# Result stores made events of their own in five buffers, and the order of all events written anew, in a fused attention and feed-forward kernel

## The chip, the cores and the metric

One core of one Trainium2 chip runs the whole program. The metric is the device time of one launch in microseconds (us), the median over several runs. Of one execution there is also a profile: what every engine (PE, DVE, ACT, POOL, SP) and every DMA queue did, and when.

## The reference

Two stages stand behind one another. The first is an attention over 8 batches, 8 heads, 576 positions and 64 channels, in a local and a coarse part that are added. The second is a feed-forward block over the 4608 = 8 x 576 tokens with 512 channels in, 2048 hidden and 512 out.

```python
q_d = q.reshape(B, H, Sd, 4, D).mean(axis=3)          # k_d and v_d likewise; Sd = 144
out_up = np.repeat(sm_attn(q_d, k_d, v_d), 4, axis=2) # softmax attention, each row four times
mask = np.abs(pos[:, None] - pos[None, :]) < 4        # the local band
scores = np.where(mask, scale * np.matmul(q, k.transpose(0, 1, 3, 2)), -1000000000.0)
attn = softmax(scores)
attn_out = out_up + np.matmul(attn, v)
x = attn_out.transpose(0, 2, 1, 3).reshape(4608, 512)
h = x @ w_in
g = np.where(h > 0.0, h, np.exp(np.minimum(h, 0.0)) - 1.0)
return g @ w_out
```

## The kernel before

The work is cut into some 1,280 small events, each a call of one short function that emits a few instructions. A table of words in the program, ORDER, lists the events in the order in which they are emitted; `run` first emits what an event depends on (its `after` list) and, where a buffer it takes is full (its `alloc` list, against the table CAP), the users of the oldest one. An engine executes its own instructions strictly in the order of emission, and waits at each for what it needs from the others. So ORDER decides what stands behind what on PE, DVE, ACT, POOL and SP.

The events' names have a letter code and indices: b is a batch of 0 to 7, j a pair of heads of 0 to 3, t a block of 512 tokens of 0 to 8, i a number within a block. For attention:

- `lq` and `lv` load q, k and v of a pair. SP issues `lq` (L321), except for batches 0 and 1, where POOL issues DMAs that also cast (L308), and SP issues the four DMAs of `lv` (L358). `cq` (L344) and `cv` (L386) cast to 16 bit on POOL, each with a tiny copy behind it (L333).
- `tr` transposes q and k of a pair on PE (L409 for batches 0 and 1, L414 after), and `eq`, `ek` evict them (L424, on ACT or DVE by a table). From batch 3 on k is transposed by a DMA instead, which SP issues: `fl` (L427).
- `sq` and `sk` sum q and k over four positions, on DVE (L443) or POOL (L447 and L452), by a table.
- `sc` are the scores (PE, L463 local, L473 coarse), `xl` and `xf` their exponentials (ACT, L483), `mk` the band's mask (DVE, L492), `dn` the denominators (PE, L508) and `rc` their reciprocal (DVE, L518).
- The reciprocals must be spread over partitions. Batches 0 to 2 do that with matmuls, `sp` (L549) and a copy `sx` (L556). Batches 3 to 7 send them through DRAM: `so` writes them out (L529, rd<-rc) and `si` reads them back spread (L535, rcb<-rd, two DMAs); SP issues both.
- `vs` and `vd` are sums of v on PE (L566) and their copy (L574), `out` and `far` the outputs on PE (L592, L611), `nm` the normalisation (DVE, L638 and L643), `ad` adds both parts into the block's input xt (L650, on POOL, or on DVE where the table `adv` says so).

For the feed-forward block:

- `m1` computes 128 hidden rows of a block, four 128x512 matmuls (L663); the first two of block 0 come in pieces, `mp`. `ex` (ACT, L683, or two passes L680 and L681 where the table `rl` says so) and `el` (DVE, L690, or L694 and L695) form the ELU into gt. `m2` are four matmuls of the second product (L708); sixteen of them make a block.
- `wi` and `wo` load a quarter each of the two weight matrices, issued by POOL (L286, L290). Quarter n of w_in serves the events `m1.0.4n` to `m1.0.4n+3` of block 0 and the same of later blocks.
- `cp` takes 128 finished rows: ACT copies them from PSUM to one of three buffers "os" (L716), and SP stores them (L718).

PE also runs matmuls on a tile of zeros, Z (L394), that compute nothing; a table `fill` says how many stand ahead of which event. PSUM gives two large slots (a third until `cf`), two "hp" for `m1` and two "misc" for `m2`, the vs and some of the denominators.

## Time and profile before

| | |
|---|---|
| time, median of 3 runs | 342.42 us (341.69 to 342.69) |
| the profiled execution's own time | 342.38 us |
| its span in the profile | 340.6 us |
| mean granted TensorE clock | 0.99 |
| PE busy in the span | 325.0 us (95%) |
| DVE, ACT, POOL busy | 230.7, 209.4, 156.5 us |

The span runs from the first to the last instruction that the profile shows; 1.78 us of the own time lie around it. "Busy" counts an engine's instructions, and a matmul stream at half the clock counts as busy too. Rows of a timeline give the start in us, the duration in us, the engine, the line of the program, the operation with its tiles, the count where neighbours are joined, and in brackets how long the engine had been idle and what released it. "SPq" is SP's queue, whose time is spent in issuing DMAs; the transfer itself goes on behind it. Rows by window give the stretch, then the busy time and count of PE, PEld, DVE, ACT and POOL, the granted clock as a share of full speed, the DMA engines' share and GB/s.

### The profile page before, as it was taken

The numbers are of one execution on the slowest core, as the hardware profiler recorded it, in microseconds if no ns is written. First come the engines' busy times: TensorE is split into PE (matmuls) and PEld (weight loads), VectorE is DVE, ScalarE is ACT, GpSimd is POOL, SyncE is SP. The second block draws the span as 40 slices with busy tenths as digits, with TensorE's granted clock in tenths as the row PEclk, the third lists the DMA queues.
The fourth block names the chain that finished last, engine by engine and source line by source line (L and its number), as shares of the span: only waits on it lengthen the run. The fifth ranks groups of instructions, "written<-read, shape, count | busy, mean of one in ns | idle before, by whom it ended". The sixth has DMA issues, their size and how long they took to land.

```text
span 340.6 us, 9762 instructions
## 1 busy us (share of the span) xinstructions
PE 325.0 (95%) x3976; PEld 169.8 (50%) x3976; DVE 230.7 (68%) x429; ACT 209.4 (61%) x365; POOL 156.5 (46%) x299
## 2 busy tenths in 40 slices
PE   6799979999999997999999999999999999999996
PEld 3355445555545553555555555555444444444443
DVE  2668998768778957788997966699775455443400
ACT  3544888888457862555676767765446646657621
POOL 6694765876795674857684347632011000000000
PEclk9879999999999999999999999999999999999999
DMA  8999999989887949999996996331310100000112
GB/s 168 195 180 227 168 248 224 196 196 155 214 149 165 232 114 179 249 199 224 166 251 152 162 239 169 115 88 69 89 64 31 63 34 31 31 33 31 56 70 92
DMA packets 99735, 48.66 MB, mean 143 GB/s; under 512 B 81130, under 2 KB 94698, under 8 KB 99690
## 3 DMA queue, kind: packets, MB, share of 16 engines
q1 hardware_dynamic: 93530, 41.57, 55.1%
q0 software_dynamic: 5600, 6.26, 11.4%
q8 instruction: 31, 0.51, 0.7%
q10 hardware_dynamic: 560, 0.21, 0.3%
q14 instruction: 14, 0.11, 0.1%
HBM read 41.66 MB, written 9.67 MB: 151 GB/s over the span
## 4 chain that ended last, share of the span: by engine, by line
PE 66%; DMA 15%; DVE 8%; ACT 3%; SPq 3%; issue 2%; POOL 1%; ACTq 0%; POOLq 0%; DVEq 0%
PE op L708 28%; PE hp L663 28%; DMA v<-in_v_dram 4%; DMA rcb<-rd 3%; DMA k<-in_k_dram 3%; DMA kt<-k 3%; DVE gt L695 2%; PE lg L592 2%; DVE rc L518 1%; SPq L427 1%; PE sc L463 1%; DVE e L694 1%; DVE ln L643 1%; DMA MASK<-MASKc 1%; PE den L508 1%
## 5 line engine op out<-in xcount | busy, mean ns | idle before, releaser
L663 PE MATMUL hp<-xt,WI 128*128 128x512 f16 x576 | 148.0, 380 | 2.5 <-DVE gt L695 2.2
L708 PE MATMUL op<-WO,gt 128*128 128x512 f16 (+2 forms) x592 | 145.3, 374 | 0.0
L663 PEld LDWEIGHTS <-WI 128*128 128x128 f16 x576 | 62.6, 114 | 57.3 <-issue 3.6
L708 PEld LDWEIGHTS <-gt 128*128 128x128 f16 x592 | 55.1, 98 | 60.2
L690 DVE SCALAR_TENSOR_TENSOR gt<-e,hp 128x512 f16<-128x512 f16 x71 | 48.4, 683 | 43.0 <-ACT e L681 42.6
L683 ACT ACTIVATE e<-hp 128x512 f16<-128x512 f32 x73 | 43.6, 599 | 41.5 <-PE hp L663 40.0
L680 ACT ACTIVATE r<-hp 128x512 f32<-128x512 f32 x71 | 42.6, 600 | 40.9 <-PE hp L663 40.5
L695 DVE SCALAR_TENSOR_TENSOR gt<-hp,e 128x512 f16<-128x512 f32 x73 | 50.5, 692 | 2.8
L650 POOL TENSOR_TENSOR xt<-ln 128x320 f16<-128x320 f16 (+7 forms) x35 | 25.8, 750 | 44.9 <-DVE ln L643 44.8
L681 ACT ACTIVATE e<-r 128x512 f16<-128x512 f32 x71 | 44.7, 630 | 2.2
L483 ACT ACTIVATE pex<-sc 128x580 f16<-128x580 f32 (+1 forms) x64 | 35.2, 591 | 11.3 <-PE sc L473 11.2
L694 DVE TENSOR_SCALAR e<-e 128x512 f16<-128x512 f16 x73 | 27.3, 374 | 20.3 <-ACT e L683 20.2
L386 POOL CAST v<-v 128x640 f16<-128x640 f32 x32 | 23.6, 738 | 13.4 <-DMA v<-in_v_dram 7.2
L716 ACT COPY os<-op 128x512 f32<-128x512 f32 (+2 forms) x37 | 21.1, 573 | 12.6 <-PE op L708 12.3
L643 DVE TENSOR_TENSOR ln<-lg,rcb 128x580 f16<-128x580 f32 x32 | 24.1, 752 | 0.0
L344 POOL CAST k<-k 96x768 f16<-96x768 f32 x24 | 19.6, 818 | 9.1 <-DMA k<-in_k_dram 9.1
L447 POOL TENSOR_TENSOR t<-qt 128x288 f32<-128x288 f16 x19 | 12.8, 672 | 23.6 <-ACT qt L424 13.1
L492 DVE TENSOR_TENSOR pex<-pex,MASK 128x580 f16<-128x580 f16 x32 | 19.6, 626 | 2.4 <-ACT pex L483 2.2
L344 POOL CAST q<-q 96x768 f16<-96x768 f32 x24 | 19.6, 817 | 0.0
L424 ACT COPY qt<-tqk 128x576 f16<-128x576 f16 x18 | 11.5, 637 | 5.9 <-PE tqk L414 5.0
L447 POOL TENSOR_TENSOR t<-kt 128x290 f32<-128x290 f16 x17 | 11.9, 703 | 6.8 <-DMA kt<-k 5.4
L638 DVE TENSOR_TENSOR ln<-lg,rcb 128x144 f16<-128x144 f32 x32 | 9.6, 300 | 7.7 <-PE lg L611 3.7
(71 smaller groups left out, 292.6 us busy)
## 6 DMA issues: line engine op xcount, KB each, us to landing
v<-in_v_dram SPq DMA_DIRECT2D x126, 80.0 KB, 4.2
out_dram<-os SPq DMA_DIRECT2D x35, 256.0 KB, 2.7
q<-in_q_dram SPq DMA_DIRECT2D x25, 288.0 KB, 4.9
k<-in_k_dram SPq DMA_DIRECT2D x25, 288.0 KB, 5.0
rcb<-rd SPq DMA_DIRECT2D x10, 362.0 KB, 5.4
WI<-in_moe_w_in_dram POOLq DMA_DIRECT2D x4, 512.0 KB, 10.7
WO<-in_moe_w_out_dram POOLq DMA_DIRECT2D x4, 512.0 KB, 7.5
q<-in_q_dram POOLq DMA_DIRECT2D x7, 144.0 KB, 6.8
```

The costliest lines, as they stand in the source:

```text
L344: nc.gpsimd.tensor_copy(out=x[:], in_=src)
L483: nc.scalar.activation(out=s["p"][:, :, a : a + n], in_=g2(s["sc"], a, n), func=AF.Exp, scale=SCALE / 16 if far else SCALE,)
L643: nc.vector.tensor_tensor(**near)
L650: eng.tensor_tensor(out=xt(t)[:, j, t0 - TBLK * t : t1 - TBLK * t], in0=ln[:, a:z], in1=_rep4(ln[:, ga : ga + (z - a) // 4]), op=AB.add,)
L663: nc.tensor.matmul(hps[(t, fc)][:], w_in(dc, fc), xts[t][:, dc, :], start=(dc == 0), stop=(dc == DMC - 1),)
L680: nc.scalar.activation(out=r[:], in_=hp[:], func=AF.Relu, scale=-1.0)
L681: nc.scalar.activation(out=e[:], in_=r[:], func=AF.Exp, scale=-1.0)
L683: nc.scalar.activation(out=e[:], in_=hp[:], func=AF.Exp)
L690: nc.vector.scalar_tensor_tensor(out=gts[t][:, fc, :], in0=e[:], scalar=-1.0, op0=AB.add, in1=hp[:], op1=AB.max)
L694: nc.vector.tensor_scalar(out=e[:], in0=e[:], scalar1=1.0, scalar2=-1.0, op0=AB.min, op1=AB.add)
L695: nc.vector.scalar_tensor_tensor(out=gts[t][:, fc, :], in0=hp[:], scalar=0.0, op0=AB.max, in1=e[:], op1=AB.add)
L708: nc.tensor.matmul(op_[:, a:z], gts[t][:, fc, 128 * tt : 128 * tt + 128], WO[fc // 4][:, fc % 4, a:z], start=(fc == 0), stop=(fc == FCN - 1),)
```

## The change

The event `cp` is split in two. `result` (still `cp`) is ACT's copy, and takes one of five buffers instead of three. `store` (a new event, `st`) is SP's DMA; ORDER places it at any later point, and a copy that takes a buffer is emitted only behind the store that frees it.

```diff
-    def store(t, i):
-        a, z = {16 * NT - 4: (0, 384), 16 * NT - 3: (384, DM)}.get(16 * t + i, (0, DM))
-        os_ = sb.tile([128, DM], FP32, tag="os", bufs=3, name="os")
+    outs = {}
+
+    def of_row(t, i):
+        return {16 * NT - 4: (0, 384), 16 * NT - 3: (384, DM)}.get(16 * t + i, (0, DM))
+
+    def result(t, i):
+        a, z = of_row(t, i)
+        os_ = outs[(t, i)] = sb.tile([128, DM], FP32, tag="os", bufs=5, name="os")
         nc.scalar.copy(out=os_[:, a:z], in_=ops.pop((t, i))[:, a:z])
+
+    def store(t, i):
+        a, z = of_row(t, i)
         r = TBLK * t + 128 * (i // 4)
-        nc.sync.dma_start(out=out[r : r + 128, a:z], in_=os_[:, a:z])
+        nc.sync.dma_start(out=out[r : r + 128, a:z], in_=outs.pop((t, i))[:, a:z])
...
-        q16=4, k16=4, q32=3, k32=3, xt=3, gt=2, rd=2, e=3,
+        q16=4, k16=4, q32=3, k32=3, xt=3, gt=2, rd=2, e=3, os=5,
...
-                at(("cp", t, n), store, t, n, after=[("m2", t, i)])
+                at(("cp", t, n), result, t, n, after=[("m2", t, i)], alloc=[("os", [("st", t, n)])])
+                at(("st", t, n), store, t, n, after=[("cp", t, n)])
```

ORDER and the tables that go with it are new throughout: 1,281 events become 1,318, the 37 stores being the difference. The table `fill` has 30 Z matmuls where it had 31, among them:

```diff
-  'fill': {('sc', 0, 0): 5,
-           ('sc', 0, 1): 3,
-           ('dn', 0, 0): 5,
-           ('sc', 0, 3): 2,
-           ('dn', 0, 1): 4,
-           ('sp', 0, 2): 2,
+  'fill': {('sc', 0, 0): 1,
+           ('dn', 0, 0): 8,
+           ('sp', 0, 0): 3,
+           ('sp', 0, 1): 2,
```

Of its Z matmuls 29 stood ahead of the first whole `m1` event and 2 behind it; now it is 22 and 8. The table `rl` (ELU in two ACT passes and one of DVE) has 59 entries where it had 71, `adv` (adds on DVE) 22 where it had 29, and the tables that give evictions, sums and copies to one engine or the other are changed for most batches.

Three places show what the new order moves. The first is POOL at the start of the program. In the rows, `t` and `ke` or `qd` are the two passes of a sum of k or q, the DMAs are loads of batch 1, and `CAST v` and `COPY apart` are a cast of batch 0's v. In the kernel before POOL has, behind the first sum of k:

```order
L447 TENSOR_TENSOR t_218<-kt 128x290
L452 TENSOR_TENSOR ke<-t_218 128x5x29
L308 DMA q_264<-in_q_dram 96x2x384
L308 DMA k_266<-in_k_dram 96x2x384
L386 CAST v_296<-v_90 128x640
L333 COPY apart<-v_296 1x1
L447 TENSOR_TENSOR t_300<-qt 128x288
L452 TENSOR_TENSOR qd<-t_300 128x144
```

In the changed kernel (whose lines are four higher here) it has:

```order
L451 TENSOR_TENSOR t_215<-qt 128x288
L456 TENSOR_TENSOR qd<-t_215 128x144
L451 TENSOR_TENSOR t_251<-qt 128x288
L456 TENSOR_TENSOR qd<-t_251 128x144
L312 DMA q_290<-in_q_dram 96x2x384
L312 DMA k_292<-in_k_dram 96x2x384
L390 CAST v_294<-v_186 128x640
L337 COPY apart<-v_294 1x1
```

The sums of q of pairs 0 and 1 now stand ahead of the loads and of the first cast of v; before, the sum of q of pair 1 stood behind that cast.

The second place is POOL where the second and the third quarter of w_in are issued, about the first events of block 0. Before:

```order
L386 CAST v_519<-v_186 128x640
L333 COPY apart<-v_519 1x1
L286 DMA WI<-in_moe_w_in_dram 128x4x512 x2
L386 CAST v_569<-v_159 128x640
L333 COPY apart<-v_569 1x1
L368 MEMSET v_600 1x1
L368 MEMSET v_606 1x1
L650 TENSOR_TENSOR xt<-ln 128x512 x3
```

In the changed kernel, with the second quarter in the first row and the third in the last:

```order
L290 DMA WI<-in_moe_w_in_dram 128x4x512
L372 MEMSET v_544 1x1
L372 MEMSET v_655 1x1
L654 TENSOR_TENSOR xt<-ln 128x512 x3
L451 TENSOR_TENSOR t_803<-qt 128x288
L456 TENSOR_TENSOR qd<-t_803 128x144
L348 CAST q_806<-q_329 96x768
L337 COPY apart<-q_806 1x1
L348 CAST k_809<-k_332 96x768
L337 COPY apart<-k_809 1x1
L290 DMA WI<-in_moe_w_in_dram 128x4x512
```

The third quarter has moved behind the three adds that complete batch 0's share of xt, one sum and one pair of casts.

The third place is SP about the spread of batch 3's reciprocals. In the kernel before, from a load of v to the row that writes the reciprocals out:

```order
L358 DMA v_2432<-in_v_dram 64x5x64 x4
L321 DMA q_2450<-in_q_dram 96x2x384
L321 DMA k_2452<-in_k_dram 96x12x64
L718 DMA out_dram<-os 128x512 x2
L358 DMA v_2517<-in_v_dram 64x5x64 x4
L321 DMA q_2579<-in_q_dram 96x2x384
L321 DMA k_2581<-in_k_dram 96x12x64
L427 DMA_TRANSPOSE kt<-k_2632 128x6x96
L427 DMA_TRANSPOSE kt<-k_2643 128x6x96
L718 DMA out_dram<-os 128x512
L358 DMA v_2674<-in_v_dram 64x5x64 x4
L529 DMA rd<-rc 128x181
```

In the changed kernel:

```order
L431 DMA_TRANSPOSE kt<-k_2429 128x6x96
L431 DMA_TRANSPOSE kt<-k_2557 128x6x96
L362 DMA v_2565<-in_v_dram 64x5x64 x4
L325 DMA q_2581<-in_q_dram 96x2x384
L325 DMA k_2583<-in_k_dram 96x12x64
L431 DMA_TRANSPOSE kt<-k_2620 128x6x96
L431 DMA_TRANSPOSE kt<-k_2483 128x6x96
L362 DMA v_2701<-in_v_dram 64x5x64 x4
L533 DMA rd<-rc 128x181
L431 DMA_TRANSPOSE kt<-k_2879 128x6x96
L539 DMA rcb<-rd 64x4x724 x2
```

The three stores and one load of v that stood between the two pairs of transposes and ahead of the reciprocals' row are gone from here; the pairs of transposes themselves stay ahead of it. One more transpose stands between the reciprocals' two rows, as it did before. For batch 5, which the prediction speaks of too, SP's order was: the row that writes the reciprocals out, three transposes, the row that reads them back; now it is three transposes, the row that writes, one transpose, the row that reads.

More of the change, by code (lines that the diff above doesn't have):

```diff
@@ L109 @@
           ('mp', 1, 0): 2,
[9 rows of a table removed]
+          ('m1', 0, 7): 1,
+          ('m1', 0, 10): 1,
+          ('sp', 1, 0): 1,
+          ('sp', 1, 2): 1,
+          ('sc', 2, 1): 1,
+          ('m1', 1, 15): 1,
+          ('sc', 3, 3): 1,
+          ('out', 3, 2): 1},
[6 rows of a table added]
  'soq': [],
@@ new lines @@
+xf.1.1 m1.0.9 ex.0.9 cv.1.2 ad.0.1.1 m1.0.10 mk.1.2 xf.1.2 tr.2.1 el.0.9 dn.1.0 ex.0.10 el.0.10 eq.2.1
+ek.2.1 cv.1.0 vs.1.0 wo.0 m1.0.11 lv.2.1 vd.1.0 rc.1.0 ex.0.11 sq.2.1 lv.2.0 sp.1.0 sp.1.2 sx.1.0 out.1.0
+sk.2.1 cq.2.3 far.1.0 m1.0.12 el.0.11 sx.1.2 ex.0.12 out.1.2 far.1.2 wo.2 nm.1.0 ad.1.0.1 sp.1.1 sx.1.1
+ad.0.3.1 m1.0.13 cq.2.0 nm.1.2 out.1.1 far.1.1 wo.1 sp.1.3 el.0.12 cv.2.2 lv.3.2 m1.0.14 nm.1.1 out.1.3
+lq.3.2 far.1.3 ex.0.13 el.0.13 ad.1.0.2 m1.0.15 xt.3 ad.1.1.1 sx.1.3 lq.3.0 nm.1.3 sc.2.1 m2.0.0 ex.0.14
@@ new lines @@
+el.5.8 el.5.9 so.6 m1.5.10 cv.7.0 xf.7.2 ex.5.10 xl.7.3 xf.7.3 lv.7.1 cp.4.4 el.5.10 ad.5.0.6 mk.7.3 m2.4.9
+m1.5.11 m2.4.10 m1.5.12 ex.5.11 out.6.0 out.6.2 far.6.0 el.5.11 ex.5.12 el.5.12 far.6.2 m2.4.11 cv.7.1
+cv.7.2 m1.5.13 m2.4.12 cp.4.8 si.6 ad.5.1.6 nm.6.0 ad.6.0.7 ad.6.0.6 mk.7.2 nm.6.2 ex.5.13 vs.7.0 vd.7.0
+dn.7.0 m1.5.14 ex.5.14 rc.7.0 out.6.1 out.6.3 far.6.1 far.6.3 m2.4.13 el.5.13 ad.6.2.6 m1.5.15 ex.5.15
+nm.6.1 xt.8 m2.4.14 ad.6.1.6 out.7.0 nm.6.3 out.7.2 ad.6.3.6 st.4.8 el.5.14 m1.6.0 ex.6.0 m2.4.15 st.3.8
@@ new lines @@
+cp.4.12 el.5.15 m1.6.1 ex.6.1 m2.5.0 el.6.0 m1.6.2 ex.6.2 far.7.2 far.7.0 so.7 st.4.0 si.7 el.6.1 el.6.2
+m1.6.3 ex.6.3 el.6.3 m2.5.1 ad.6.1.7 m1.6.4 m2.5.2 ex.6.4 ad.6.2.7 nm.7.2 m1.6.5 ex.6.5 el.6.4 m2.5.3
+st.3.12 cp.5.0 st.5.0 nm.7.0 el.6.5 m1.6.6 m2.5.4 ex.6.6 m1.6.7 ex.6.7 st.4.4 el.6.6 el.6.7 m2.5.5 m1.6.8
+ex.6.8 el.6.8 m2.5.6 m1.6.9 m2.5.7 out.7.3 out.7.1 far.7.3 far.7.1 ad.6.3.7 nm.7.1 m2.5.8 m1.6.10 m2.5.9
+ex.6.9 ex.6.10 el.6.9 m1.6.11 m2.5.10 cp.5.4 ex.6.11 el.6.10 ad.7.2.7 m1.6.12 ex.6.12 st.5.4 m2.5.11
```

186 lines of the change are left out of this document (86 added, 100 removed), and 15 rows, old and new, of the table CFG.

## The prediction

> **What bounds the kernel now.** I read the page's head first, then the table of windows, then the timeline where the windows show PE idle.
>
> ```profile
> span 340.6 us, 9762 instructions
> PE 325.0 (95%) x3976; PEld 169.8 (50%) x3976; DVE 230.7 (68%) x429; ACT 209.4 (61%) x365; POOL 156.5 (46%) x299
> ```
>
> PE is the bound: 325.0 of 340.6 us, with DVE next at 68%. An order can win only what PE loses to idle time or to a low clock. The windows (stretch; busy time and count of PE, PEld, DVE, ACT, POOL; granted clock; DMA share; GB/s) tell where that is:
>
> ```profile
> 10.00:20.00 10.00, 7.71 (x162) 4.16 (x158) 5.67 (x9) 4.46 (x9) 6.78 (x14) 0.72 1.35 196
> ...
> 40.00:50.00 10.00, 7.85 (x177) 4.85 (x171) 9.64 (x21) 8.36 (x16) 7.06 (x16) 1.00 1.06 231
> ...
> 110.00:120.00 10.00, 9.36 (x171) 5.05 (x169) 9.42 (x12) 8.45 (x16) 6.03 (x12) 1.00 1.10 220
> 120.00:130.00 10.00, 9.09 (x157) 4.89 (x155) 6.86 (x12) 7.01 (x14) 7.53 (x14) 1.00 0.61 142
> 130.00:140.00 10.00, 8.70 (x146) 4.34 (x146) 7.36 (x15) 1.71 (x4) 5.03 (x7) 1.00 0.98 176
> ...
> 260.00:270.00 10.00, 10.00 (x48) 4.94 (x47) 4.86 (x10) 7.31 (x13) 1.32 (x2) 1.00 0.07 26
> ```
>
> From 260 on PE is full and nothing can be won there except by taking matmuls away. Between 110 and 140 it is idle for 0.64 + 0.91 + 1.30 = 2.85 us, and before 50 it loses most: 2.29 idle in 10 to 20 at a clock of 0.72, and 2.15 in 40 to 50, where DVE is busy for 9.64 of 10 us. So three things decide: the start, batch 3, and whether the new order opens a hole in the full part.
>
> **The start.** This is the path to the first denominators (PE, L508) in the kernel before:
>
> ```profile
> 8.31 0.45 PE L409 MATMUL tqk<-ID,k 96*64 96x96 f16 x12 [0.45 <-DMA k<-in_k_dram]
> ...
> 8.69 1.25 PE L394 MATMUL sc<-Z 128*128 128x512 f16 x5
> 9.59 0.64 ACT L424 COPY kt<-tqk 128x576 f16<-128x576 f16 x1 [1.77 <-DVE qt L424]
> 10.26 0.76 DVE L443 TENSOR_REDUCE ke<-kt 128x145 f16<-128x580 f16 x1
> ...
> 12.64 0.45 PE L409 MATMUL tqk<-ID,k 96*64 96x96 f16 x12 [0.86 <-DMA k<-in_k_dram]
> 13.12 0.82 POOL L386 CAST v<-v 128x640 f16<-128x640 f32 x1 [2.82 <-issue]
> 14.15 0.65 POOL L447 TENSOR_TENSOR t<-qt 128x288 f32<-128x288 f16 x1
> 14.88 0.42 POOL L452 TENSOR_TENSOR qd<-t 128x144 f16<-128x144 f32 x1
> 15.36 0.40 PE L473 MATMUL sc<-qd,ke 64*64 64x144 f16 x8 [1.24 <-POOL v L368]
> 15.69 2.32 PE L394 MATMUL den<-Z 128*128 128x512 f16 x5
> 15.80 1.07 ACT L483 ACTIVATE pex<-sc 128x580 f16<-128x580 f32 x2 [1.50 <-PE sc L473]
> 16.49 0.50 DVE L492 TENSOR_TENSOR pex<-pex,MASK 128x580 f16<-128x580 f16 x1 [1.39 <-ACT pex L483]
> 17.93 1.04 PE L508 MATMUL den<-pex,IND 128*32 128x181 f16 x20
> ```
>
> The cast of v at 13.12 is late, and the sum of q of pair 1 (14.15, then 14.88 to 15.30) stands behind it on POOL. The coarse scores need that sum, and PE gets to them at 15.36. In the changed order that sum stands ahead of the cast. Pair 1 is transposed at 8.31 + 0.45 = 8.76; two ACT copies of 0.64 make 10.04, DVE's sum of k 0.76 more, so its scores can run from 10.8, some 4.5 us sooner. Exponentials (2 x 1.07, first behind the eviction of pair 3) and mask (0.50) then end by about 14.
>
> That isn't all won, because PE's own queue is next: behind the transposes of pair 2 (12.64 + 0.45 = 13.1) the table `fill` now puts 8 Z matmuls ahead of the denominators. One costs 2.32 / 5 = 0.46 us at half clock and 1.25 / 5 = 0.25 at full clock. So the denominators start at 13.1 + 3.7 = 16.8, or at 13.1 + 2.0 = 15.1, against 17.93: 1.1 or 2.8 us sooner. Behind them, up to the first whole `m1`, stand 13 Z matmuls where there were 16 (29 less the 13 of the first three entries; now 22 less 9), another 3 x 0.25 = 0.75. So the feed-forward part starts 1.85 to 3.55 us sooner. Which clock it will be, these windows tell only for the old order:
>
> ```profile
> 10.00:15.00 5.00, 3.07 (x99) 1.93 (x96) 3.43 (x6) 3.01 (x6) 2.04 (x5) 0.95 1.36 206
> 15.00:20.00 5.00, 4.64 (x63) 2.23 (x62) 2.24 (x4) 1.45 (x3) 4.74 (x10) 0.50 1.33 186
> ```
>
> PE was busy 3.07 of 5 us to 15, and ran at 0.50 after that. The changed order has four Z matmuls fewer in that stretch, so I expect a drop there too, and take 2.5, about a third of the way from the cold end to the warm one. The first exponential of the feed-forward part then comes at 30.05:
>
> ```profile
> 32.55 1.09 ACT L683 ACTIVATE e<-hp 128x512 f16<-128x512 f32 x2 [3.39 <-PE hp L663]
> ...
> 43.88 1.02 PE L663 MATMUL hp<-xt,WI 128*128 128x512 f16 x4 [0.58 <-DVE gt L695]
> ```
>
> Of these 2.5 us, 6 x 0.25 = 1.5 are given back, since 8 Z matmuls stand behind the first `m1` where there were 2. Those 8 lie partly in holes of PE and partly on its path; I count them all. **Term 1: -1.0**, with bounds of -2.05 (3.55 less 1.5) and, if the DVE-bound stretch of 40 to 50 takes all, 0.
>
> [...]
>
> **Batch 3.** The reciprocals go to DRAM and back by SP:
>
> ```profile
> 114.82 4.36 SPq L427 DMA_TRANSPOSE kt<-k  x2
> ...
> 116.49 1.29 DVE L518 RECIPROCAL rc<-den 128x181 f16<-128x181 f32 x1
> ...
> 119.27 0.53 SPq L718 DMA_DIRECT2D out_dram<-os  x1
> 119.85 4.10 SPq L358 DMA_DIRECT2D v<-in_v_dram  x4
> ...
> 124.05 0.56 SPq L529 DMA_DIRECT2D rd<-rc  x1
> ...
> 124.72 1.22 SPq L427 DMA_TRANSPOSE kt<-k  x1
> ...
> 126.25 1.25 SPq L535 DMA_DIRECT2D rcb<-rd  x2
> ...
> 132.72 0.31 DVE L638 TENSOR_TENSOR ln<-lg,rcb 128x144 f16<-128x144 f32 x1 [2.44 <-DMA rcb<-rd]
> ...
> 133.75 0.35 PE L592 MATMUL lg<-pex,v 64*64 64x58 f16 x20 [0.99 <-DVE ln L643]
> ...
> 134.63 0.35 PE L592 MATMUL lg<-pex,v 64*64 64x58 f16 x20 [0.31 <-DVE ln L643]
> ```
>
> The reciprocal is done at 117.78, but SP is held up behind transposes, a store and four loads of v, and sends it 6.3 us later. DVE waits 2.44 us for it, and PE 0.99 + 0.31. In the changed order, between the first pair of transposes (the one ahead of 114.82) and the second stand 6 DMAs instead of 11 (8 loads of v, 4 of q and k and 2 stores make 14; now 4 and 2). At some 0.6 us each (0.53 for the store, 4.10 / 4 for v) the eight that went make about 5 us, and the store of 119.27 is gone too. I take 4 us of it, since the transposes may themselves wait for their casts, which go with POOL and not with SP. Against it, PE's lead is shorter: one `m1` (1.02) and one `sc` (its coarse part was 0.40 at half clock in the row of 15.36; with the local part I estimate 0.6) fewer stand between the denominators and the output that needs the result, 1.6 us. So the result comes 4 - 1.6 = 2.4 us sooner relative to its use, as much as DVE's wait of 2.44. The 1.30 of PE's idle goes, and some 0.5 of the slow first matmuls behind each gap (an estimate): **term 2: -1.8**. Bounds: all the idle time of 110 to 140 goes, -2.85; or the transposes wait as long as before and only the shorter lead counts, +1.0.
>
> **Buffers and stores.** This row (busy and mean ns, then the engine's idle time ahead of it and what ended it) is the copy to "os":
>
> ```profile
> L716 ACT COPY os<-op 128x512 f32<-128x512 f32 x35 | 20.3, 585 | 10.1 <-PE op L708 9.9 <-DMA k<-in_k_dram 0.3
> ```
>
> ACT never waited for a store: 9.9 of its 10.1 us of idle time end with PE's own matmul. So five buffers remove no wait; their use is only that SP may issue a store later. What that can cost: one copy of block 2 stands behind a store that SP reaches behind two transposes, 0 to 1.5 (a transposing issue takes 1.22); I take **+0.2**. At the end a store that could go earlier is issued behind a later one, one issue of 0.53 at most; **+0.2**. The fewer two-pass ELUs and adds on DVE move work between engines that are not the bound in the full part, so 0 there, covered by PE's 10.00 of 10 us in 260 to 270; if DVE loses its slack in 40 to 50, it is the next paragraph's second case.
>
> The sum against the profiled execution's own 342.38: -1.0 - 1.8 + 0.2 + 0.2 = -2.4, so **340.0 us**. The median of the runs, 342.42, is 0.04 above that execution and changes nothing.
>
> **The rivals.** A is the forecast.
>
> B: the gains are eaten. DVE in 40 to 50 (9.64 of 10 us) sets the pace whatever comes before, and batch 3's transposes wait for their casts. Terms 1 and 2 are 0, and 342.38 + 0.4 less the one Z matmul is some 342.5. Against it: PE has idle time at both places that the rows put down to other waits. That the change does nothing it says (five buffers that no copy needs) ends here too.
>
> [...]
>
> D: slower, by the third quarter of w_in.
>
> ```profile
> 23.30 1.52 POOL L286 DMA_DIRECT2D WI<-in_moe_w_in_dram  x2
> ...
> 28.08 3.26 POOL L650 TENSOR_TENSOR xt<-ln 128x512 f16<-128x512 f16 x3 [2.22 <-DVE ln L643]
> ...
> DMA to landing us min/median/max: 7.3/10.7/14.2
> ```
>
> Before, POOL issued it by 24.8, and `m1.0.8` used it at 43.88, long after it landed. Now it stands behind the three adds, a sum and two casts. The adds ended at 31.34, so at 28.84 if all is 2.5 sooner; a sum (0.65 + 0.42), two casts with their copies (about 1.0 each, 0.82 of it the cast) and some gaps put its issue at 32.2. It lands at 39.5, 42.9 or 46.4. The event that needs it comes at 43.88 less about 2, so 42. It decides from there: at the median it costs 0.9, at the longest 4.4, and the time is 344.4 (or 340.9). For it: the DMA share is still 1.06 in 40 to 50. Against it: the shortest landing costs nothing.
>
> E: slower too, by the same queue at batch 5. There the new SP order has three transposes ahead of the reciprocals' row and one between the two; the old one sent that row first. By the waits of SP's queue a transpose waits for POOL's cast (us, times, longest):
>
> ```profile
> SPq L427 <- POOL apart L333: 8.5, 7, 1.5
> ```
>
> That is 1.2 us each, 3.6 for three, and the time is 343.6 if no other PE work covers it.
>
> **How the numbers follow.** A 0.43, C 0.07: both faster. B 0.17: no change. D 0.20 and E 0.13: slower. A change of 0.3% (1.0 us) is about what a measurement of this kernel can tell from none; so faster (under 341.4) 0.50, within 0.17, slower (over 343.45) 0.33. The forecast is A's 340.0. The range goes from 337.5 (A with both terms near their lower bounds, -2.05 and -2.85) to D's 344.4.
>
> **What would show it.** In the changed profile: the denominators of pair 0 near 16 to 17 us and the first exponential of the feed-forward part near 30 (term 1); the reciprocals of batch 3 written out within 3 us of the DVE row, and no idle time of PE ahead of L592's successor behind a normalisation there (term 2); ACT's copy to "os" waiting for a DMA (the buffers). The prediction is wrong if `m1.0.8` waits for a DMA, if 178 to 200 shows PE idle ahead of outputs, or if a window behind 140 has PE under 9.5 where it was full.

## The result and the profile after

The changed kernel takes 342.86 us (median of 21 runs, 339.56 to 347.19) against 342.79 us (21 runs, 339.97 to 345.85) for the kernel before on the same chip. The ratio is 1.0006, with a 95% interval of 0.9983 to 1.0029: no difference that can be measured. The forecast was 340.0 us. Runs of one and the same kernel spread over several us here; so in what follows the place of an effect is read from profiles, and its size is believed where several executions or a ratio bear it out.

The head of the page after:

```profile
span 340.8 us, 9741 instructions
## 1 busy us (share of the span) xinstructions
PE 325.2 (95%) x3975; PEld 169.8 (50%) x3975; DVE 229.4 (67%) x432; ACT 206.7 (61%) x360; POOL 156.7 (46%) x296
```

Span and PE's sum are as before (340.6 and 325.0), but PE's idle time lies elsewhere. These are the windows of the changed kernel (columns as in the prediction):

```profile
10.00:20.00 10.00, 9.01 (x212) 5.28 (x213) 7.63 (x14) 7.02 (x15) 7.75 (x16) 0.83 1.21 190
20.00:30.00 10.00, 7.93 (x169) 4.60 (x167) 6.00 (x14) 2.98 (x5) 6.56 (x13) 0.76 1.20 211
30.00:40.00 10.00, 8.47 (x102) 4.25 (x100) 7.04 (x15) 5.87 (x11) 8.32 (x15) 0.90 1.13 184
40.00:50.00 10.00, 9.02 (x216) 5.64 (x216) 9.61 (x23) 9.21 (x19) 6.13 (x12) 1.00 1.16 235
...
60.00:70.00 10.00, 9.00 (x77) 4.93 (x65) 6.48 (x14) 6.57 (x13) 5.43 (x10) 1.00 1.15 228
...
80.00:90.00 10.00, 8.96 (x117) 4.55 (x117) 7.59 (x11) 4.41 (x8) 5.72 (x13) 1.00 0.70 155
...
110.00:120.00 10.00, 10.00 (x171) 5.43 (x173) 8.51 (x16) 8.61 (x16) 7.14 (x16) 1.00 0.69 139
120.00:130.00 10.00, 10.00 (x179) 5.46 (x172) 8.99 (x16) 5.43 (x10) 2.72 (x6) 1.00 0.51 112
130.00:140.00 10.00, 9.83 (x184) 4.96 (x186) 8.92 (x17) 6.27 (x13) 5.39 (x9) 1.00 1.02 174
...
170.00:180.00 10.00, 8.49 (x127) 4.33 (x127) 9.81 (x16) 6.35 (x13) 7.86 (x16) 1.00 1.16 227
```

And those windows of the kernel before that the prediction did not show:

```profile
20.00:30.00 10.00, 9.52 (x245) 5.75 (x244) 7.36 (x21) 6.18 (x12) 7.53 (x15) 0.93 1.19 208
30.00:40.00 10.00, 9.49 (x149) 5.24 (x147) 9.18 (x19) 6.71 (x13) 5.71 (x11) 1.00 1.13 180
...
60.00:70.00 10.00, 9.72 (x75) 5.49 (x74) 7.26 (x12) 8.46 (x16) 7.60 (x15) 1.00 1.07 182
...
80.00:90.00 10.00, 9.96 (x175) 5.50 (x174) 8.68 (x16) 6.00 (x11) 5.20 (x12) 1.00 0.98 189
...
170.00:180.00 10.00, 10.00 (x142) 5.20 (x141) 9.53 (x17) 7.12 (x14) 8.73 (x18) 1.00 0.90 238
```

Adding ten less the first busy number of each window gives PE's idle time by stretch:

| stretch | idle before | idle after | difference |
|---|---|---|---|
| 0 to 60 us | 8.47 | 8.84 | +0.37 |
| 60 to 110 | 0.47 | 2.15 | +1.68 |
| 110 to 140 (batch 3) | 2.85 | 0.17 | -2.68 |
| 140 to 200 | 0.82 | 1.57 | +0.75 |
| 200 to 340 | 2.38 | 2.11 | -0.27 |

So the change did win at one place what was expected there, and more; the same amount was lost at others.

**Batch 3** lost its stall, as the prediction had it. The rows of the changed kernel:

```profile
119.86 0.66 PE L512 MATMUL den<-pex,IND 128*32 128x181 f16 x40
...
122.11 1.28 DVE L522 RECIPROCAL rc<-den 128x181 f16<-128x181 f32 x1
...
123.42 0.36 SPq L533 DMA_DIRECT2D rd<-rc  x1
...
125.98 1.25 SPq L539 DMA_DIRECT2D rcb<-rd  x2
...
132.50 0.30 DVE L642 TENSOR_TENSOR ln<-lg,rcb 128x144 f16<-128x144 f32 x1
```

The reciprocal ends at 123.39, and SP sends it 0.03 us later instead of 6.3. The last row has no bracket: DVE no longer waits for rcb, and PE is idle for 0.17 us between 110 and 140 instead of 2.85. Of the 2.85 only 1.30 stood behind these normalisations; the rest were smaller waits for other things, which went too. The whole reciprocal comes 5.6 us later than before (122.11 against 116.49), and its row leaves only 0.6 us sooner (123.42 against 124.05), while DVE gets to the normalisation at 132.50 where it stood ready at 130.28 before. By these rows the stall went because SP was free when the reciprocal came, and because the use came later.

**The start** came out differently. Its rows after:

```profile
12.86 2.89 PE L398 MATMUL den<-Z 128*128 128x512 f16 x8
...
15.68 0.65 PE L512 MATMUL den<-pex,IND 128*32 128x181 f16 x20
...
22.26 0.72 POOL L390 CAST v<-v 128x640 f16<-128x640 f32 x1 [1.44 <-DMA v<-in_v_dram]
...
23.03 0.30 PE L570 MATMUL vs<-v,VR 128*32 128x128 f16 x8 [1.41 <-POOL v L390]
...
32.73 0.60 ACT L687 ACTIVATE e<-hp 128x512 f16<-128x512 f32 x1 [6.37 <-PE hp L667]
...
34.73 1.89 PE L667 MATMUL hp<-xt,WI 128*128 128x512 f16 x8 [0.66 <-DVE gt L699]
```

The denominators start at 15.68, within the 15.1 to 16.8 of the prediction and 2.25 us sooner than before. But then PE waits for the last cast of v, which waits for its load. In ORDER this load, `lv.0.1`, stood third of batch 0's four and is now the last; before, no cast of v waited for a load there. Windows of 2.5 us show the clock behind that wait:

```profile
20.00:22.50 2.50, 1.63 (x33) 1.01 (x31) 1.35 (x2) 1.47 (x3) 1.06 (x4) 1.00 1.06 223
22.50:25.00 2.50, 1.97 (x44) 1.08 (x44) 0.91 (x1) 0.75 (x2) 2.10 (x5) 1.00 1.19 213
25.00:27.50 2.50, 1.83 (x60) 1.26 (x64) 2.08 (x7) 0.76 (x1) 1.77 (x5) 0.53 1.31 212
27.50:30.00 2.50, 2.50 (x37) 1.25 (x38) 1.67 (x7) 0.00 (x0) 1.62 (x2) 0.50 1.26 195
30.00:32.50 2.50, 2.50 (x9) 0.98 (x8) 1.66 (x5) 0.00 (x0) 2.42 (x4) 0.61 1.24 204
```

After 1.4 us of idle time in 20 to 25 the granted clock falls to 0.5 a second time, for some 7 us. The first exponential of the feed-forward part starts at 32.73 (before: 32.55; forecast: 30.05).

**Three new holes** make up the rest. Each row names what PE waited for:

```profile
63.90 1.02 PE L712 MATMUL op<-WO,gt 128*128 128x512 f16 x4 [1.00 <-DMA WO<-in_moe_w_out_dram]
...
79.95 2.78 DVE L496 TENSOR_TENSOR pex<-pex,MASK 128x580 f16<-128x580 f16 x3
...
84.06 0.66 PE L512 MATMUL den<-pex,IND 128*32 128x181 f16 x40 [1.04 <-DVE gt L699]
...
174.87 1.23 DVE L654 TENSOR_TENSOR xt<-ln 128x320 f16<-128x320 f16 x1
...
177.08 1.02 PE L667 MATMUL hp<-xt,WI 128*128 128x512 f16 x4 [0.64 <-DVE gt L699]
...
179.38 1.02 PE L667 MATMUL hp<-xt,WI 128*128 128x512 f16 x4 [0.69 <-DVE gt L699]
```

At 63.90 it is a quarter of w_out that hadn't landed: the new order has POOL issue the third quarter (53.01) ahead of the second (56.27), and the second `m2` needs the second. At 84.06 it is DVE, with three masks in a row ahead of an ELU. At 177 and 179 it is DVE again, busy for 9.81 of 10 us.

Nothing came of the stores, either way. The page's row of the copies:

```profile
L725 ACT COPY os<-op 128x512 f32<-128x512 f32 (+2 forms) x37 | 20.9, 571 | 13.6 <-PE op L712 13.6
```

All of ACT's idle time ahead of them still ends with PE.

### The profile page after: what moved, and what is told of

Same layout as the page of the kernel before. It is cut to its first block, busy times and chain, and to the rows that moved or that the text cites. A ratio compares the mean times of both kernels' runs of the same rounds, so it can differ in the third digit from the quotient of the medians.

```text
span 340.8 us, 9741 instructions
## 1 busy us (share of the span) xinstructions
PE 325.2 (95%) x3975; PEld 169.8 (50%) x3975; DVE 229.4 (67%) x432; ACT 206.7 (61%) x360; POOL 156.7 (46%) x296
## 4 chain that ended last, share of the span: by engine, by line
PE 72%; DMA 15%; DVE 7%; SPq 3%; ACT 1%; issue 1%; POOL 0%; POOLq 0%; DVEq 0%
PE op L712 33%; PE hp L667 30%; DMA v<-in_v_dram 12%; SPq L362 3%; DMA WO<-in_moe_w_out_dram 2%; PE tqk L418 2%; PE lg L596 2%; DVE pex L496 2%; DVE ln L647 1%; PE sc L467 1%; DVE gt L699 1%; DVE e L698 1%; DMA q<-in_q_dram 1%; PE vs L570 1%; PE den L512 1%
## 5 line engine op out<-in xcount | busy, mean ns | idle before, releaser
L687 ACT ACTIVATE e<-hp 128x512 f16<-128x512 f32 x85 | 50.9, 600 | 57.5 <-PE hp L667 55.4
L694 DVE SCALAR_TENSOR_TENSOR gt<-e,hp 128x512 f16<-128x512 f16 x59 | 40.4, 684 | 40.5 <-ACT e L685 40.0
L699 DVE SCALAR_TENSOR_TENSOR gt<-hp,e 128x512 f16<-128x512 f32 x85 | 58.8, 692 | 3.1
L654 POOL TENSOR_TENSOR xt<-ln 128x512 f16<-128x512 f16 (+7 forms) x42 | 30.4, 736 | 56.8 <-DVE ln L647 56.6
L684 ACT ACTIVATE r<-hp 128x512 f32<-128x512 f32 x59 | 35.3, 598 | 27.7 <-PE hp L667 27.5
L698 DVE TENSOR_SCALAR e<-e 128x512 f16<-128x512 f16 x85 | 31.0, 365 | 30.0 <-ACT e L687 29.5
L685 ACT ACTIVATE e<-r 128x512 f16<-128x512 f32 x59 | 37.2, 631 | 1.9
L451 POOL TENSOR_TENSOR t<-qt 128x288 f32<-128x288 f16 x17 | 11.8, 693 | 34.1 <-ACT qt L428 31.2
L428 ACT COPY qt<-tqk 128x576 f16<-128x576 f16 x23 | 14.6, 640 | 7.3 <-PE tqk L418 4.8
L447 DVE TENSOR_REDUCE ke<-kt 128x145 f16<-128x580 f16 x18 | 13.5, 748 | 2.7 <-ACT kt L428 2.6
```

Source lines behind the costliest of these rows:

```text
L654: eng.tensor_tensor(out=xt(t)[:, j, t0 - TBLK * t : t1 - TBLK * t], in0=ln[:, a:z], in1=_rep4(ln[:, ga : ga + (z - a) // 4]), op=AB.add,)
L684: nc.scalar.activation(out=r[:], in_=hp[:], func=AF.Relu, scale=-1.0)
L685: nc.scalar.activation(out=e[:], in_=r[:], func=AF.Exp, scale=-1.0)
L687: nc.scalar.activation(out=e[:], in_=hp[:], func=AF.Exp)
L694: nc.vector.scalar_tensor_tensor(out=gts[t][:, fc, :], in0=e[:], scalar=-1.0, op0=AB.add, in1=hp[:], op1=AB.max)
L698: nc.vector.tensor_scalar(out=e[:], in0=e[:], scalar1=1.0, scalar2=-1.0, op0=AB.min, op1=AB.add)
```

## The experiments

The ratios are to the kernel before on the same chip, with 95% intervals; the changed kernel's own is 1.0006.

### What each new hole costs

**e2_wo_order.** The two words are exchanged in ORDER:

```diff
-sk.2.1 cq.2.3 far.1.0 m1.0.12 el.0.11 sx.1.2 ex.0.12 out.1.2 far.1.2 wo.2 nm.1.0 ad.1.0.1 sp.1.1 sx.1.1
-ad.0.3.1 m1.0.13 cq.2.0 nm.1.2 out.1.1 far.1.1 wo.1 sp.1.3 el.0.12 cv.2.2 lv.3.2 m1.0.14 nm.1.1 out.1.3
+sk.2.1 cq.2.3 far.1.0 m1.0.12 el.0.11 sx.1.2 ex.0.12 out.1.2 far.1.2 wo.1 nm.1.0 ad.1.0.1 sp.1.1 sx.1.1
+ad.0.3.1 m1.0.13 cq.2.0 nm.1.2 out.1.1 far.1.1 wo.2 sp.1.3 el.0.12 cv.2.2 lv.3.2 m1.0.14 nm.1.1 out.1.3
```

> The changed kernel with the words of the second and the third quarter of w_out exchanged in the order, so that POOL issues the second quarter at 53.0 in place of 56.3 us. Theory T: the second m2, which waited 1.00 us for that quarter at 63.90, waits for nothing (the quarter took 7.6 us, so it lands near 60.6), PE is busy for 10.0 of 10 us in 60 to 70 less what other waits leave, and the end is 0.8 to 1.1 us sooner. Rival S: the wait turns into another one within 20 us, and the end is the same within 0.3.

Measured: 339.67 us, ratio 0.9949 (0.9915 to 0.9982). Its window:

```profile
60.00:70.00 10.00, 10.00 (x92) 5.36 (x91) 7.43 (x15) 7.37 (x14) 6.46 (x11) 1.00 1.12 210
```

T holds: PE is full there, and the kernel is 0.57% (1.9 us) below the changed one. That is more than the 1.00 us of the one profile. In the other executions without this edit the same wait is 1.27 (e1), 1.69 (e3), 2.31 (e4), 1.49 (e7) and 1.73 us (e13), so the profile of the changed kernel shows the shortest of them. In all seven with the edit (e2, e8, e10, e12, e14, e15, e16) PE has 10.00 of 10 us in this window.

**e4_rl.** Five more entries in `rl`, one fewer in `adv`:

```diff
-  ... [3, 0, 3], [3, 0, 4], [4, 2, 5], [4, 3, 5], ...
+  ... [3, 0, 3], [3, 0, 4], [4, 3, 5], ...
...
-  ... [3, 12], [3, 14], [4, 3], ...
+  ... [3, 12], [3, 13], [3, 14], [3, 15], [4, 0], [4, 1], [4, 2], [4, 3], ...
```

> The changed kernel with five more ELUs (blocks 3 and 4, about 169 to 180 us) in two ACT passes and one of DVE, and one add taken from DVE to POOL. Theory T (the new tables made DVE the bound at 163 to 179: its chain lies unbroken on the path there, and PE is idle for 1.51 us in 170 to 180): DVE has about 5 x 0.38 + 0.48 = 2.4 us less to do, PE is busy for at least 9.8 of 10 us in 170 to 180 in place of 8.49, and the end is 1.2 to 1.6 us sooner. Rival S (ACT, which gets 5 x 0.63 = 3.2 us more, becomes the bound): PE's idle time stays above 1 us and is put down to ACT, and the end is the same or later.

Measured: 341.37 us, ratio 0.9992 (0.9952 to 1.0031). The time alone doesn't decide; the place is read in the next kernel, which has this edit too.

**e8_wo_rl.** e2's and e4's edits together.

> The changed kernel with the two edits together that closed a hole each: the second quarter of w_out issued ahead of the third, and five more two-pass ELUs and one add fewer on DVE at 169 to 180 us. Theory T (the holes are independent and what they cost stays gained): the second m2 waits for nothing, PE is busy for 9.8 of 10 us or more in 170 to 180, and the kernel is 2.5 to 4 us faster than the changed kernel, so 338.5 to 340, faster than both. Rival S (what is gained at 64 is lost again before 180): the same as the run with the w_out edit alone.

Measured: 339.32 us, ratio 0.9907 (0.9873 to 0.9942). Its window of batch 5:

```profile
170.00:180.00 10.00, 9.84 (x83) 4.84 (x82) 6.02 (x10) 7.96 (x15) 6.86 (x15) 1.00 0.86 175
```

PE has 9.84 of 10 us where it had 8.49, and DVE 6.02 where it had 9.81. All seven executions with this edit (e4, e8, e10, e12, e14, e15, e16) have 9.84 or more there; of the six without it, five have 8.45 to 8.76, and in e13, which runs later, the idle time lies in 180 to 190 (8.61). The kernel is 1% below the changed one (3.4 us), and below the kernel before. That 1.35 us of it are the tables' is read from this window; the ratio's own step from e2 (0.9949) to here lies within the intervals.

**e16_again.** The same kernel again, under another label.

> The kernel with the w_out edit and the five more two-pass ELUs once more, unchanged. Theory T (the edits are worth 2.5 us or more against the kernel before): a ratio to the kernel before of 0.990 to 0.994, as in its first run (0.9907). Rival N (its first run was a lucky one; the two kernels that contain it and one edit more gave 0.996 and 0.997): a ratio of 0.995 or more. Its start shows whether the second drop of the clock comes in this execution too.

Measured: 339.01 us, ratio 0.9923 (0.9889 to 0.9957). T holds: by the two runs the edits are worth 2.8 to 3.4 us against the changed kernel.

**e11_before_tables.** The other way round: the kernel before with the changed kernel's `rl` and `adv`, all of them.

> The kernel before with two tables of the changed one: which ELUs go in two ACT passes (59 in place of 71), and which adds run on DVE (22 in place of 29); the order stays. Theory T (the prediction's price of nothing for these tables was wrong: DVE, at 9.2 to 9.5 of 10 us in 160 to 180, becomes the bound there): PE loses 1 to 2 us more in 150 to 200 than before, and the kernel is 0.5 to 2 us slower than before. Rival V (the tables only cost together with the new order): PE stays at 9.9 of 10 us or more in 170 to 180, and the end is the same within 0.3%.

Measured: 349.35 us over 6 runs (345.52 to 350.64), ratio 1.0185 (1.0134 to 1.0237). Slower, by over three times the upper end of what T had. In its profile, of its shortest run (345.52 us), PE is busy for 9.59 of 10 us in 150 to 160 and 9.27 in 180 to 190, where the kernel before had 10.00 in both. But in 160 to 180, where T looked, PE has 10.00, and where most of the 6 us go this profile doesn't show. So these tables are far from free; they fit the order that they were made with, and even there not everywhere.

**e3_dn2.** One copy and four matmuls are put ahead of batch 2's denominators:

```diff
-dn.2.0 ex.1.12 cq.3.2 fl.3.2 cp.0.0 m2.0.8 el.1.12 rc.2.0 ...
+ex.1.12 cq.3.2 fl.3.2 cp.0.0 m2.0.8 dn.2.0 el.1.12 rc.2.0 ...
```

> The changed kernel with one copy of results and the four matmuls of the m2 behind it put ahead of batch 2's denominators instead of behind them. Theory T (PE stood 1.04 us at 84.06 because the denominators wait for DVE, which has three masks in a row ahead of the last ELU): the four matmuls fill that hole, PE is idle there for at most 0.4 us, and the end is 0.6 to 1.2 us sooner. Rival S (DVE is late anyhow, and the same time is lost at the next ELU): the hole moves behind 86 us, and the end is the same within 0.3.

Measured: 342.19 us, ratio 1.0016 (0.9986 to 1.0047). The rows:

```profile
82.24 1.02 PE L712 MATMUL op<-WO,gt 128*128 128x512 f16 x4 [0.40 <-ACT os L725]
...
85.25 0.47 PE L553 MATMUL rb<-rc,FOUR 8*128 8x181 f16 x4 [0.42 <-DVE rc L522]
```

S holds as to the time: one hole of 1.04 became two of 0.40, behind a copy of ACT, and 0.42, behind DVE's reciprocal, and nothing was won.

**e14_casts_later.** e8's kernel, with two casts on POOL moved away from beside those masks:

```diff
-... m2.0.11 lq.3.3 cq.3.1 fl.3.1
+... m2.0.11 lq.3.3
...
-... lq.4.3 sx.2.1 out.2.1 far.2.3 cv.3.3 cv.3.1 sk.3.2 ...
+... lq.4.3 sx.2.1 out.2.1 far.2.3 cv.3.3 cv.3.1 cq.3.1 fl.3.1 sk.3.2 ...
```

> The kernel with the w_out edit and the five more two-pass ELUs, with one pair of casts of batch 3 (and its transpose on SP) moved on POOL from 80.5 to 82.4 us to behind two casts of v that wait for their loads to about 86, so that POOL is idle beside the three masks on DVE. Theory T (a mask takes 0.42 us alone and 0.92 beside a cast, and that decides the hole of PE at 84): the three masks take 1.3 to 1.9 us in place of 2.8, and PE is idle for under 0.2 us in 80 to 90, in this execution as in any. Rival X (the masks are slow for another reason, and POOL's wait in the executions without the hole was a coincidence): they take 2.5 us or more with POOL idle. The end is given back in part if the moved transpose is late: from 0.5 us faster to 1 us slower.

Measured: 339.10 us, ratio 0.9933 (0.9907 to 0.9960). Its masks, and those of e1, where POOL's cast of k happened to wait for its load just then:

```profile
78.91 1.62 DVE L496 TENSOR_TENSOR pex<-pex,MASK 128x580 f16<-128x580 f16 x3
```

```profile
79.40 1.27 DVE L496 TENSOR_TENSOR pex<-pex,MASK 128x580 f16<-128x580 f16 x3
...
80.32 1.02 POOL L348 CAST k<-k 96x768 f16<-96x768 f32 x1 [0.35 <-DMA k<-in_k_dram]
```

T holds for the masks: the same three take 2.78 us beside two casts (2.77 in e3, e4 and e13), 1.90 with one of the two beside them (e7), 1.62 with an add of POOL there instead (e14), and 1.27 where POOL was waiting for the load of k (e1, e2, e8, e12, e15, e16). In those six PE is busy for 9.99 or 10.00 of 10 us in 80 to 90. In e14 the wait at the denominators is gone, but 0.48 us come back at a later output, behind a copy of DVE, so that T's 0.2 us for this window is missed. The kernel as a whole is the same as e16. So this hole is in some executions of the changed kernel's order and not in others, as POOL has to wait for its load of k there (0.23 to 1.40 us in those six) or not.

**e10_mask.** e8's kernel with `mk.2.0` moved ahead of `sq.2.2`, from a place at 80 us to one at about 72.

> The kernel with the w_out edit and the five more two-pass ELUs, and one mask of batch 2 moved on DVE from 80 us to about 72, so that two masks and not three stand in a row ahead of the last ELU before the denominators. Theory T (a mask takes 0.42 us alone and 0.92 beside a cast on POOL; three beside casts made PE wait 1.04 us at 84): the hole at 84 stays under 0.3 us even where casts stand beside the masks, and the kernel is 0 to 1 us faster than the one without this edit, since that one had the hole in some executions and not in others. Rival S (DVE has no slack at 72 either): PE idle appears between 70 and 80, and the end is the same or later.

Measured: 340.68 us, ratio 0.9958 (0.9927 to 0.9990). S: PE is busy for 9.47 of 10 us in 70 to 80, where it waits twice for DVE (0.22 and 0.30), and 9.57 in 80 to 90, where 0.43 us of the hole remain. DVE had no slack ahead of it either.

### The start

**e1_more_z.** Seven more Z matmuls about 18 to 23 us:

```diff
-  'fill': {..., ('dn', 0, 0): 8, ('sp', 0, 0): 3, ('sp', 0, 1): 2, ...
+  'fill': {..., ('dn', 0, 0): 8, ('dn', 0, 1): 2, ('sp', 0, 0): 3, ('sp', 0, 1): 7, ...
```

> The changed kernel with seven more Z matmuls in its idle stretch of 18 to 23 us (2 ahead of the second denominators, 5 more ahead of the spread of pair 1); nothing else is changed. Theory T (the start lost its gain to a second drop of the clock, which the idle time of 20 to 25 brought on): the granted clock of 25 to 32.5 is above 0.9 in place of 0.53, 0.50 and 0.61, and the first whole m1 behind the two in pieces starts near 33 us in place of 34.73; at the end the kernel is 0.5 to 2 us faster than the changed kernel. Rival R (the loads of v set the pace there, not the clock): the clock is mended, but that m1 starts within 0.5 us of 34.73. Rival S (DVE, full from 40 to 50, takes it all back): that m1 is sooner, yet the events near 53 us come as before, and the end is the same or later by the seven matmuls.

Measured: 342.11 us, ratio 1.0011 (0.9978 to 1.0045): the same. The clock is 1.00 from 20 to 35 us, and the `m1` that T and R speak of starts at 33.87, which is 0.86 sooner, but not near 33. The clock was mended as T had it, and the median shows no gain. The seven matmuls can't be what ate it in this execution: the last cast of v ends at 23.63, and PE starts on it at 23.77. Up to 59 us its events stay 0.80 to 0.87 sooner, then the wait for w_out is 0.27 longer. Why the time of the runs is the same stays open.

**e15_four_z.** e8's kernel with four more, where PE waits for the last cast of v (`('sp', 0, 1): 6` in place of 2).

> The kernel with the w_out edit and the five more two-pass ELUs, with four more Z matmuls ahead of the spread of pair 1 at about 21 us, where PE waits for the last cast of v. Theory T (the second drop of the clock costs the start 1.5 to 2 us in the executions that have it, and PE's idle time at 20 to 24 brings it on): no half clock between 24 and 33 us, the first whole m1 by 33.5, and 0.5 to 1.5 us faster than without them. Rival V (four times 0.216 us on PE's path weigh as much as the clock): the same within 0.3%.

Measured: 338.41 us over 6 runs, ratio 0.9887 (0.9854 to 0.9921), the lowest of all, though its interval overlaps those of e8 and e16. The clock of this execution and of e16's, in 25 to 27.5 us:

```profile
25.00:27.50 2.50, 2.34 (x85) 1.40 (x87) 2.11 (x5) 1.64 (x4) 0.15 (x1) 1.00 1.27 198
```

```profile
25.00:27.50 2.50, 2.50 (x62) 1.59 (x60) 0.99 (x3) 0.56 (x1) 0.69 (x4) 0.50 1.26 212
```

No second drop with the four, a long one without; but this is one execution of each. In e15's the last cast of v was done at 22.09, and PE got to it only at 24.27, behind the four: it had no wait to fill there, and the `m1` starts at 34.37, not by 33.5. e3 and e7 have neither more Z matmuls nor a drop, so the drop is not in every execution of the changed order.

What the drop costs can be counted from the sums of the last v (`vs`, 23.03 in the changed kernel) to that `m1` (34.73). In e3:

```profile
22.76 0.30 PE L570 MATMUL vs<-v,VR 128*32 128x128 f16 x8
...
32.86 1.89 PE L667 MATMUL hp<-xt,WI 128*128 128x512 f16 x8 [0.85 <-DVE gt L699]
```

That is 10.10 us, and it is 10.10 in each of the six executions without a second drop (e1, e3, e7, e12, e13, e15). With a drop it is 11.1 to 11.7 us (11.70 in the changed kernel; e2, e4, e8, e10, e14), and 13.20 in e16, where the clock is low from some 20 to 34 us. So the drop costs 1.0 to 1.6 us, and 3.1 in e16. The rest of what differs between executions comes from where the last `vs` start: at 22.76 to 24.27 us, and later in e12 and e13, whose starts were changed.

**e13_sum_back.** The changed kernel, with the sum of q of pair 1 put back behind the first cast of v:

```diff
-xt.2 ek.0.1 sq.0.0 sc.0.0 xl.0.0 sq.0.1 lv.0.1 sk.0.1 xf.0.0 sc.0.1 lq.1.0 cv.0.2 tr.0.3 ...
+xt.2 ek.0.1 sq.0.0 sc.0.0 xl.0.0 lv.0.1 sk.0.1 xf.0.0 lq.1.0 cv.0.2 sq.0.1 sc.0.1 tr.0.3 ...
```

> The changed kernel with one part of the start undone: the sum of q of pair 1 stands on POOL behind the load of batch 1 and the first cast of v again, as before the change. Theory T (the earlier denominators of pair 0 were worth nothing, since the loads of v gate what comes behind them): the denominators start 1 to 3 us later than 15.7, yet the m1 that stood at 46.0 comes within 0.7 us of it, and the time is the same within 0.3%. Rival G (the earlier denominators were worth what the prediction gave them, and other things ate it): that m1 and the end are 1 to 2.5 us later.

Measured: 345.18 us over 6 runs, ratio 1.0085 (1.0054 to 1.0115), 2.7 us above the changed kernel. The denominators:

```profile
20.82 0.65 PE L512 MATMUL den<-pex,IND 128*32 128x181 f16 x20
```

They come 5.1 us later, more than intended, and the `m1` of 46.0 comes at 48.30. G holds for that size. Yet over the executions of the changed order the denominators start anywhere from 13.94 (e8) to 17.42 us (e4), and the `m1` that follows them at 34.73 comes at 34.11 and 34.61, with 32.86 for 16.88 (e3): no relation. The rows show why. Where no cast holds them up, the last `vs` start 5.88 us behind the denominators (16.88 and 22.76 in e3, 20.82 and 26.70 here). In most of the others they start as the last cast of v ends, which is at 22.1 to 24.1 us by the execution. So being early is worth something down to 16 to 18 us, and nothing below that.

**e12_v_act.** e8's kernel with one of batch 0's loads of v issued by ACT at the very start.

> The kernel with the w_out edit and the five more two-pass ELUs, with the four loads of v of batch 0's pair 1 issued by ACT at the very start instead of as the last of seventeen by SP. Theory T (the first outputs wait for the last v, which POOL casts at 22.3 us in the kernels before and after alike, because SP issues its load at 16.4): the last cast of batch 0 starts by 19.5, the first whole m1 comes 1.5 to 3 us sooner than 34 to 35, and the end is 0.5 to 2 us sooner. Rival D (the DMA engines, at a share over 1 there, set the pace): the last cast starts within 1 us of 22.3, and the end is the same.

Measured: 340.83 us, ratio 0.9974 (0.9944 to 1.0004). Neither: the last cast of batch 0 comes at 24.02, later than 22.3, and the denominators at 18.94, since ACT issues those four loads ahead of its first copies (its first cast starts at 8.16 in place of 4.10 in e8). In the kernel before the last cast of v starts at 24.81; the 22.3 that the expectation gives for it is its third. Whether loads of v that come sooner would help stays open.

**e7_no_late_z.** Without the six single Z matmuls behind 42 us (`m1.0.7`, `m1.0.10`, `sc.2.1`, `m1.1.15`, `sc.3.3`, `out.3.2`).

> The changed kernel without the six single Z matmuls that stand ahead of two m1 of block 0, one of block 1, two scores and one output (42 to 140 us). Theory T (they are on PE's path and give the gain of the start back): 6 x 0.216 = 1.3 us faster than the changed kernel, 0.6 to 1.3 allowing for those that lie in holes. Rival V (they stand where PE is idle, or hold the clock): the same within 0.3, or slower with a granted clock under 1.00 somewhere behind 40 us.

Measured: 342.63 us, ratio 1.0025 (0.9991 to 1.0059), the same within what can be told. V by the time; the clock stays at 1.00 from 40 to 330 us without them, so it isn't the clock that they hold.

### Batch 3 and the buffers

**e5_before_so3.** One edit of the kernel before: one load of v stands behind the spread of batch 3 instead of ahead of it.

```diff
-... cp.1.4 m1.2.10 el.2.9 lv.5.0 dn.3.0 rc.3.0 ... vs.3.0 so.3 ... si.3 m1.2.13 ...
+... cp.1.4 m1.2.10 el.2.9 dn.3.0 rc.3.0 ... vs.3.0 so.3 ... si.3 lv.5.0 m1.2.13 ...
```

> The kernel before, with one load of v (four DMAs, 4.1 us of SP) moved from ahead of batch 3's reciprocals on SP to behind the rows that read them back; nothing else is changed. Theory T (SP's queue was what held batch 3 up): the row that writes the reciprocals out comes within 3 us of the DVE row instead of 6.3 behind it, PE's idle time of 110 to 140 falls from 2.85 to under 1.2, and the kernel is 1.5 to 2.5 us faster than before. Rival U (the transfer itself, 5.7 us in the chain of waits, or the shorter cover sets it): the row is early, but PE's idle time stays over 2 us and the end is the same.

Measured: 342.23 us, ratio 0.9995 (0.9959 to 1.0030): the same. The rows tell why:

```profile
118.65 0.61 SPq L529 DMA_DIRECT2D rd<-rc  x1
...
130.60 0.31 DVE L638 TENSOR_TENSOR ln<-lg,rcb 128x144 f16<-128x144 f32 x1 [2.50 <-DMA rcb<-rd]
...
131.63 0.35 PE L592 MATMUL lg<-pex,v 64*64 64x58 f16 x20 [1.02 <-DVE ln L643]
...
140.00 0.72 POOL L386 CAST v<-v 128x640 f16<-128x640 f32 x1 [3.98 <-DMA v<-in_v_dram]
...
142.63 0.41 PE L566 MATMUL vs<-v,VR 128*32 128x128 f16 x16 [1.16 <-POOL v L386]
```

And two pieces of the chain of waits, the reciprocals' way to DRAM and back:

```profile
118.65 5.32 DMA rd<-rc
...
124.65 5.83 DMA rcb<-rd
```

The reciprocals leave at 118.65, 5.4 us sooner than before and 1.3 behind the DVE row, so SP's queue did hold that row up. But the stall behind it is still there: DVE waits 2.50 us for rcb where it waited 2.44, and PE 1.02 and 0.31 where it had 0.99 and 0.31. The write now takes 5.32 us to land (2.19 before), so that the data are back only 2.1 us sooner (130.48 against 132.59), and DVE is ready 2.2 us sooner as well. PE's idle time of 110 to 140 does fall from 2.85 to 1.33, but what went are the smaller waits for other things; the 1.33 are this stall. So U has it right at this place, the transfer, if not in its number, and an early row alone doesn't remove the stall. Besides, the load that was moved comes late itself: POOL waits 3.98 us for v, PE 1.16 and 0.49 for POOL, and the window of 140 to 150 has 8.35 us of PE where it had 9.88. Which of its moves rid the changed kernel of the stall, no run shows by itself.

**e9_split_only.** The kernel before with the split and five buffers, each `st` directly behind its `cp`.

> The kernel before with the split alone: copy and store are two events, five buffers, every store directly behind its copy, the order otherwise as before. Theory T (no copy ever waited for a store): the same as before within 0.3%. Rival W (the buffers themselves matter): 0.5 us or more either way, and ACT's idle time ahead of the copies changes.

Measured: 342.50 us, ratio 1.0035 (0.9999 to 1.0072). Not faster. Whether it is slower by 0.3% the interval leaves open; its profile has ACT's 13.0 us ahead of the copies ending with PE, all of it.

## Why the prediction was wrong

**Term 2 (batch 3) was right** in place, and its balance of an earlier row against a shorter lead is borne out by the rows of the changed kernel: the row leaves 6.2 us sooner behind the reciprocal (4 were taken), and the use comes 3.4 us sooner behind it (1.6 were taken), so 2.8 net for 2.4. That the net came so close is partly luck. Its picture of SP's queue as the one cause is not borne out: in e5 the row was early and the stall stayed. Forecast was -1.8; the idle time of 110 to 140 fell by 2.68, of which 1.13 are at the two waits that the term named, and no run shows its 0.5 for slow first matmuls. (The 11 DMAs of that step are a slip; its sum uses 14.)

**Term 1 (the start) failed** at its second step, and that is the step that made the forecast wrong together with the terms that it lacked. The denominators came as computed. "So the feed-forward part starts 1.85 to 3.55 us sooner" did not follow: the first `m1` in pieces came at 29.54 instead of 30.37, and the exponential behind it at 32.73 instead of 32.55. Two things stood between. The last cast of v, at 22.26, waits for its load, which the new order itself issues last, so what PE saved ahead of it became idle time. And the step counted the Z matmuls that were taken away as time saved, where PE's idle time in their place was followed by a second drop of the clock in 7 of the 9 profiled executions of this start without Z matmuls added (all but e3 and e7). In the changed kernel's profile the drop is worth 1.6 us: without it that `m1` would have come at some 33.1 (an estimate, 23.03 + 10.10) against 34.25 before, 1.1 us sooner and still less than the 1.85 us of the forecast's lower end. Rival C, that the clock comes back early, did come true at 15 us (0.66 in 10 to 15, 1.00 from there to 25), and still gave nothing.

**"So 0 there" for the tables was wrong.** The cover named for it was PE's 10.00 of 10 us in 260 to 270, a stretch in which DVE has half its time free. But the fewer two-pass ELUs stand at 168 to 180 too, where DVE had 9.18 and 9.53 of 10 us in the kernel before. They cost 1.35 us there (e8). With the old order they cost some 6 us in all (e11), though not at that place. The table of windows showed DVE's 9.18 and 9.53 ahead of time. The last of the prediction's own signs of being wrong came true here: a window behind 140, 170 to 180, fell from 10.00 to 8.49.

**The wait for w_out was missed.** Rival D asked what a later third quarter of w_in would do and found no more than a chance of harm; `m1.0.8` came at 43.69 against 43.88, so nothing happened. The same question was not put to w_out, two quarters of which had changed places in the same queue of POOL. It cost 1.00 us in the profile, 1.27 to 2.31 in five others, and 1.9 us by e2's ratio.

**The hole at 84 us** is in the changed kernel's profile and in some other executions only. It comes from masks on DVE that take 0.92 us beside casts on POOL and 0.42 us without. Nothing in the prediction spoke of it.

**The small terms.** No copy waited for a store, and the end of the program is as before (2.11 us idle in 330 to 340 against 2.32), so the 0.4 us taken for buffers and tail were not there. Rival E did not come: 180 to 190 has PE at 10.00, and the transposes ahead of batch 5's reciprocals were through before those were ready. Rival B's time was near the truth (342.5), for the wrong reason: the stall of batch 3 did go, and other holes took its place.

What stays open: why the clock drops a second time in some executions of one and the same start and not in others, and which move of the new order ended the stall of batch 3.

## What to carry to other kernels

When an order is made anew, a won stall is only half of the sum. Go through every queue for pieces that changed places with each other (the quarters of a weight matrix or the loads of one batch), and look up when each is first used. Judge work that moves onto an engine by the busiest window into which it falls, not by the engine's share over the whole span. And before counting an earlier start as gain, find the next thing that the stage waits for: here a load of v that the new order had put behind the others.
